# One fixed VectorE order behind attention, with weight conversion in portions, and a row of its own for token maxima

## The chip, the cores and the metric

The kernel runs on one core of one Trainium2 chip. The metric is the device time of one execution in microseconds (us), from three runs of the kernel before.

## The reference

Rotary attention over 4 batches, 8 heads, 576 positions and 64 dimensions gives 2304 tokens of 512 values; two feed-forward layers follow, here called expert 1 and expert 2 (512 to 2048 to 512). Cut to what matters:

```python
def _moe_ref(x, w_in, w_out, s, b):
    h = x @ w_in
    r = np.maximum(h, 0.0)
    g = s * (r * r) + b
    return (g @ w_out).astype(np.float32)

def _moe2_ref(x, w_in, w_out):
    h = x @ w_in
    g = h * (1.0 / (1.0 + np.exp(-1.702 * h)))
    return (g @ w_out).astype(np.float32)

def reference(**kwargs):
    attn_out = _attn_ref(**attn_kwargs)
    B, H, S, D = attn_out.shape
    x = np.ascontiguousarray(attn_out.transpose(0, 2, 1, 3)).reshape(B * S, H * D)
    x = _moe_ref(x=x, **moe_kwargs)
    return _moe2_ref(x=x, **moe2_kwargs)
```

The weights come as 64-bit floats and are turned into 32-bit ones on the chip.

## The kernel before, in words

**Stages.** Attention runs in 144 slots (to about 755 us); passes 0 to 7 of expert 1 are woven into it. `widen` (L1191) then frees attention's memory, and the rest, with which the change deals, follows: pass 8 of expert 1 (256 tokens, 755 to 805 us), pass 9 of expert 1 (512 tokens, 805 to 910 us, `LAST0` in the code), passes 10 to 13 of expert 2 (512 tokens each) and pass 14 (256 tokens, from 1295 us).

**Expert 1.** A pass has 16 blocks f of 128 hidden units. `first_layer` (L708) makes twelve matmuls into a bank `l`, then per 256 columns: ScalarE Relu from the bank (L723), VectorE times the bank again (L724: r*h, which is r*r), ScalarE scale and bias (L725), ScalarE copy to the high part (L726), VectorE subtraction for the low part (L727). `second_part` (L870) multiplies both parts into the `acc` banks two blocks later.

**Expert 2.** A pass has eight groups g of two blocks. `seven` (L816) computes both first-layer blocks with seven half-size products of half-precision pairs (a Strassen scheme): products 0, 3, 4, then 1, 2, 5, 6 with three or more `acc` matmuls in between (`between`, L1009). VectorE adds the products up (`add`, L836, tiles `u` and `c`; c1 is the half that is finished first), and product 6 is written into a bank that the sum after product 2 must have read. `gate` (L839) is ScalarE tanh (L842), VectorE multiply (L843), ScalarE copy (L844), VectorE subtraction (L845). The gate of the second half is put off into the next group (`then`, L1021).

**The next pass's tokens.** `sums_step` (L805), called once a group (in pass 9 once a block, f 5 to 12), prepares pass n+1: step 0 loads the tokens (`xr`), steps 1 and 2 take maxima on VectorE (L744, L752) and, in `share_top` (L556), store 128 maxima to memory (`tops`) and load them back as a row on all partitions (`top`), step 4 reduces that row and makes the scales (`scales`, L563 to L571, and L758) and lets GpSimd form differences, steps 5 to 7 split the result into half-precision pairs `xc` (L799 on ScalarE, L801 on VectorE). The row is a tile of the pair of buffers "r" that `seven` uses too, for `p` and `u`:

```python
row = moe.tile([128, TB], F32, tag="r", name=f"top{n}", bufs=2)
nc.sync.dma_start(row[:, 0:128], tops[n].partition_broadcast(128))
```

**Weight conversion of expert 2.** 32 raw tiles of 128x512 64-bit words (16 of each weight) go through three buffers "stage". `to_f32` (L480) costs one ScalarE operation (L483) and three VectorE operations (L484, L485, L488). `combine` (L590) takes two raw tiles to the seven weight matrices of a group: four GpSimd operations (L605), four ScalarE (L614), four VectorE (L615). `outer_pair` (L618) takes two raw tiles of the other weight: ScalarE copy (L630), GpSimd subtraction (L631) each. `refill` (L950) starts one whole such job after a block or group, in a fixed list of 16 jobs, when the buffer of expert 1's weights that it is to overwrite is free.

**What sets the order.** TensorE's order is written out (`pin`). VectorE, ScalarE, GpSimd and SP (the queue that issues all loads and stores, in order) get their order from the scheduler, which goes by priorities, readiness and free buffers; each engine then executes in that order and waits at the first instruction that is not ready. Through attention, 32 loads and maxima of expert 2's first weight (`top_load`, `top_max`, L544 to L554) are put into slots by the list `TOPS` (L1164).

## Time and profile before

| | us |
|---|---|
| three runs | 1346.38, 1350.62, 1354.55 |
| median | 1350.62 |
| the profiled execution, device time | 1356.49 |
| its span in the trace | 1354.7 |

The profiled execution is 5.9 us above the median and 1.8 us above its own span. The page gives each engine's busy time; the trace behind it lists instructions with start, length and what ended the idle time before. PE is TensorE, PEld its weight loads, DVE VectorE, ACT ScalarE, POOL GpSimd, SP the queue for transfers. A matmul of 512 columns is listed with its pipeline, so lengths of neighbours overlap.

### The profile page before, as it was taken

The numbers are of one execution on the slowest core, as the hardware profiler recorded it, in microseconds if no ns is written. First come the engines' busy times: TensorE is split into PE (matmuls) and PEld (weight loads), VectorE is DVE, ScalarE is ACT, GpSimd is POOL, SyncE is SP. The second block draws the span as 40 slices with busy tenths as digits, with TensorE's granted clock in tenths as the row PEclk, the third lists the DMA queues.
The fourth block names the chain that finished last, engine by engine and source line by source line (L and its number), as shares of the span: only waits on it lengthen the run. The fifth ranks groups of instructions, "written<-read, shape, count | busy, mean of one in ns | idle before, by whom it ended". The sixth has DMA issues, their size and how long they took to land.

```text
span 1354.7 us, 22515 instructions
## 1 busy us (share of the span) xinstructions
PE 1135.9 (84%) x8160; PEld 966.3 (71%) x8160; DVE 847.8 (63%) x1917; ACT 715.3 (53%) x1483; POOL 345.5 (26%) x363
## 2 busy tenths in 40 slices
PE   2665766898799799988999799786799797998998
PEld 1444555888798789988998797564576675776775
DVE  4978567785667665665664645889555464464554
ACT  1665665575666556665665555765333242342333
POOL 3547562153144144411111203335001001000000
PEclk9866888898899999999999899998899899999999
DMA  6687468697688766766652645544002002001010
GB/s 152 186 221 221 119 198 286 220 310 230 187 243 256 248 184 204 213 193 216 193 157 78 202 133 145 176 136 144 18 1 63 3 1 65 1 15 36 1 32 17
DMA packets 142879, 193.15 MB, mean 143 GB/s; under 512 B 32816, under 2 KB 105776, under 8 KB 142768
## 3 DMA queue, kind: packets, MB, share of 16 engines
q1 hardware_dynamic: 142768, 191.71, 47.3%
q8 instruction: 65, 1.06, 0.3%
q14 instruction: 46, 0.38, 0.1%
HBM read 146.05 MB, written 38.54 MB: 136 GB/s over the span
## 4 chain that ended last, share of the span: by engine, by line
PE 46%; DMA 19%; DVE 15%; ACT 4%; issue 4%; POOL 1%; SPq 1%; DVEq 0%; ACTq 0%; POOLq 0%
PE acc L99 20%; PE l L99 17%; DMA top<-in_moe_w_in_dram 5%; PE av L99 3%; DMA raw<-in_moe_w_in_dram 3%; PE s L99 3%; PE t L99 3%; DMA tops<-xm 2%; DVE P L394 2%; DMA stages<-in_moe_w_in_dram 1%; DMA top<-tops 1%; DVE pt L437 1%; DMA vm<-in_v_dram 1%; DVE wc L615 1%; DVE g L727 1%
## 5 line engine op out<-in xcount | busy, mean ns | idle before, releaser
L99 PE MATMUL acc<-wo,g 128*128 128x512 f32 x864 | 255.8, 422 | 5.7 <-DVE g L845 3.9
L99 PE MATMUL l<-xc,wc 128*128 128x256 f16 (+1 forms) x1680 | 203.4, 266 | 40.5 <-DVE c L836 25.7
L414 POOL TENSOR_SCALAR P<-P,st 128x576 f32<-128x576 f32 x144 | 120.4, 837 | 382.1 <-DVE st L413 251.0
L99 PEld LDWEIGHTS <-wc 128*128 128x128 f16 x1680 | 139.3, 99 | 107.7 <-issue 94.6
L99 PEld LDWEIGHTS acc<-wo,g 128*128 128x128 f32 x864 | 152.8, 195 | 34.6 <-DVE g L845 7.0
L99 PE MATMUL acc<-g,w 128*128 128x256 f32 (+1 forms) x1056 | 164.6, 306 | 5.3 <-DVE g L727 3.5
L99 PEld LDWEIGHTS acc<-g,w 128*128 128x128 f32 x1056 | 145.6, 197 | 13.0 <-DVE g L727 5.0
L403 ACT ACTIVATE P<-P,st 128x576 f32<-128x576 f32 x144 | 111.8, 776 | 78.2 <-DVE P L394 77.9
L99 PE MATMUL t<-ident,P 128*128 128x128 f32 x720 | 113.6, 293 | 44.1 <-POOL P L414 17.6
L394 DVE TENSOR_SCALAR_CACHE_REDUCE P<-s 128x576 f32<-128x576 f32 x144 | 108.3, 752 | 65.5 <-PE s L99 61.1
L99 PE MATMUL l<-xh,w 128*128 128x256 f32 x616 | 128.9, 292 | 13.5 <-DVE r L724 11.2
L842 ACT ACTIVATE r<-c 128x512 f32<-128x512 f32 (+1 forms) x80 | 47.0, 588 | 153.9 <-DVE c L836 125.7
L99 PEld LDWEIGHTS t<-ident,P 128*128 128x128 f32 x720 | 87.7, 151 | 54.9 <-POOL P L414 26.8
L99 PEld LDWEIGHTS l<-xh,w 128*128 128x128 f32 x616 | 103.6, 195 | 15.9 <-DVE r L724 14.8
L437 DVE TENSOR_TENSOR pt<-t,pt 128x640 f16<-128x640 f32 x120 | 98.4, 820 | 23.8 <-ACT pt L435 23.2
L435 ACT CAST pt<-t 128x640 f16<-128x640 f32 x144 | 98.8, 686 | 23.1 <-PE t L99 22.6
L725 ACT ACTIVATE r<-r,sb 128x256 f32<-128x256 f32 x144 | 86.6, 602 | 46.0 <-DVE r L724 45.7
L99 PE MATMUL s<-k,qb 128*128 128x320 f32 x480 | 89.2, 313 | 9.8 <-DVE P L394 8.5
L99 PE MATMUL l<-xl,w 128*128 128x256 f32 x308 | 88.4, 287 | 0.0
L727 DVE TENSOR_TENSOR g<-r,g 128x256 fp32r<-128x256 f32 x144 | 69.5, 482 | 28.6 <-ACT g L726 25.9
L99 PEld LDWEIGHTS s<-k,qb 128*128 128x128 f32 x480 | 73.9, 196 | 17.9 <-DVE P L394 10.6
L843 DVE SCALAR_TENSOR_TENSOR r<-r,c 128x512 f32<-128x512 f32 (+1 forms) x80 | 52.2, 653 | 44.6 <-ACT r L842 44.6
(145 smaller groups left out, 2025.6 us busy)
## 6 DMA issues: line engine op xcount, KB each, us to landing
ws<-wd SPq DMA_DIRECT2D x80, 512.0 KB, 4.6
k<-ksp SPq DMA_DIRECT2D x24, 576.0 KB, 6.0
top<-in_moe_w_in_dram SPq DMA_DIRECT2D x32, 256.0 KB, 3.8
raw<-in_moe_w_in_dram SPq DMA_DIRECT2D x16, 512.0 KB, 5.1
rawo<-in_moe_w_out_dram SPq DMA_DIRECT2D x16, 512.0 KB, 3.3
wd<-w SPq DMA_DIRECT2D x10, 512.0 KB, 5.0
nat<-in_k_dram SPq DMA_DIRECT2D x16, 288.0 KB, 4.5
nat<-in_q_dram SPq DMA_DIRECT2D x16, 288.0 KB, 4.7
```

The costliest lines, as they stand in the source:

```text
L99: pin(nc.tensor.matmul(*args, **kw))
L394: nc.vector.tensor_scalar(pr, ps[:, 192 : 192 + S], -Q_SCALE, None, op0=ALU.mult, op1=ALU.min, accum_out=st[:, 0:1],)
L403: nc.scalar.activation(pr, pr, AF.Exp, bias=st[:, 0:1], scale=-1.0, accum_out=st[:, 1:2])
L414: nc.gpsimd.tensor_scalar(pr, pr, st[:, 2:3], 1.0, op0=ALU.mult, op1=ALU.mult)
L435: nc.scalar.copy(hi, pc)
L437: nc.vector.tensor_tensor(lo, pc, hi, op=ALU.subtract)
L615: nc.vector.scalar_tensor_tensor(lo, src, col, hi, op0=ALU.mult, op1=ALU.subtract)
L725: nc.scalar.activation(r, r, AF.Identity, bias=sb[:, 1:2], scale=sb[:, 0:1])
L727: nc.vector.tensor_tensor(gl[:, cols], r, f32(gh[:, cols]), op=ALU.subtract)
L842: nc.scalar.activation(r, c, AF.Tanh, scale=0.851)
L843: nc.vector.scalar_tensor_tensor(r, r, 1.0, c, op0=ALU.add, op1=ALU.mult)
```

## The change

- **VectorE's order.** From `widen` on, every VectorE instruction is chained in the order in which the code is written (`dv`), with no semaphore. ScalarE's part of a conversion is kept behind the last chained one (`pace`).
- **Conversion in portions.** `combine` and `outer_pair` become generators that hand out a cost after each VectorE operation; `convert(budget)` takes portions: 1.8 per block of pass 8, 3.5 per block of pass 9, and 2.5, 0.8 and 1.5 at three places of each group. Raw tiles are loaded ahead, up to three alive (`fill`); an outer pair's job starts only when its buffer is free.
- **Token maxima.** The row is now 256 half-precision columns at the end of the tile `xc`, allocated at step 0; `sums_step` moves into the group, behind the sum after product 4.
- **Gates.** The second gate is no longer put off; it multiplies in place (c, not r).
- **Square.** In passes 8 and 9 the product L724 becomes a ScalarE Square.
- **Attention.** The 32 maxima loads go to every third slot from 40 to 133; the row of the weights' maximum moves from the buffers "r" to "V".

```diff
+    def dv(ins):
+        if late:
+            pin(ins, "dve")
+        return ins
...
-        nc.scalar.activation(f32(high), f32(high), AF.Copy, scale=2.0**-112)
-        nc.vector.tensor_scalar(low, low, 29, None, op0=ALU.logical_shift_right)
+        pace(nc.scalar.activation(f32(high), f32(high), AF.Copy, scale=2.0**-112))
+        dv(nc.vector.tensor_scalar(low, low, 29, None, op0=ALU.logical_shift_right))
+        yield 0.55
...
-    def share_top(n, col):
+    def share_top(n, col, row):
         nc.sync.dma_start(tops[n], col)
-        row = moe.tile([128, TB], F32, tag="r", name=f"top{n}", bufs=2)
-        nc.sync.dma_start(row[:, 0:128], tops[n].partition_broadcast(128))
-        return row
+        nc.sync.dma_start(row, tops[n].partition_broadcast(128))
...
+    def fill():
+        for job in [r for r in raws if "t" not in r]:
+            if live[0] == 3:
+                return
+            g, i, m = job["at"]
+            job["t"] = late["m2"].tile([128, 512], U64, tag="stage", name=f"raw{m}{g}{i}", bufs=3)
+            stage_load(job["t"], w_in2, w_out2, 2 * g + i, m)
+            live[0] += 1
...
-            nc.vector.tensor_tensor(r, r, ps[:, cols], op=ALU.mult)
+            if late:
+                nc.scalar.activation(r, r, AF.Square)
+            else:
+                nc.vector.tensor_tensor(r, r, ps[:, cols], op=ALU.mult)
...
+        xc = late["m2"].tile([128, 14 * T + 256], F16, tag="xc", name=f"xc{n}", bufs=2)
+        x["xc"] = xc[:, 0 : 14 * T].rearrange("p (j z t) -> p j z t", j=7, z=2)
+        x["row"] = xc[:, 14 * T : 14 * T + 256].bitcast(F32)
...
         add(cb[:, half:T], b1, u2)
-        then()
+        side(0)
         between()
...
         add(cb[:, half:T], a1, cb[:, half:T])
+        side(1)
         between()
         product(5, b1, False, True)
         add(cb[:, 0:half], b1, u2)
-        ready_b(*gate(cb, 1))
+        gb = gate(cb, 1)
         between()
         product(6, a1, False, True)
         add(ca[:, half:T], a1, u2)
-        return lambda: gate(ca, 0)
+        low(gb, cb)
+        ga = gate(ca, 0)
+        low(ga, ca)
+        side(2)
+        return ga, gb
...
+            if late:
+                convert(3.5 if T == 512 else 1.8)
...
+                def side(i):
+                    if i == 0 and n + 1 < len(PASSES):
+                        sums_step(ahead.setdefault(n + 1, {}), n + 1, g)
+                    convert((2.5, 0.8, 1.5)[i])
...
-    TOPS = [*range(58, 68), *range(94, 104), *range(122, 134)]
-    for i, x in enumerate(TOPS):
-        at(x, top_load, i)
-        at(x + 2, top_max, i)
+    for i in range(32):
+        at(40 + 3 * i, top_load, i)
+        at(42 + 3 * i, top_max, i)
```

**Where instructions move.** Names carry pass and group: u11_4 belongs to pass 11, group 4; the last digit of c11_41 is 1 for the half that is finished first.

VectorE, pass 11, before: the reduction of the row (L564) stands in group 2, in front of the sum after product 2 (c11_21 from l12).

```order
L752 TENSOR_REDUCE xm12_11423<-xm12_11423 128x1
L836 SCALAR_TENSOR_TENSOR u11_2_11524<-l10_8998,xm11_10634,p11_2_11523 128x256
L843 SCALAR_TENSOR_TENSOR r11_10_11546<-r11_10_11546,c11_10_11426 128x512
L836 SCALAR_TENSOR_TENSOR c11_21_11522<-l11_8999,xm11_10634,u11_2_11524 128x256
L845 TENSOR_TENSOR g11_10_11547<-r11_10_11546,g11_10_11547 128x512
L564 TENSOR_REDUCE xm12_11423<-top2_11614 128x1
L565 TENSOR_SCALAR xm12_11423<-xm12_11423 128x1
L566 TENSOR_SCALAR xm12_11423<-xm12_11423 128x1
L836 SCALAR_TENSOR_TENSOR c11_21_11522<-l12_9000,xm11_10634,c11_21_11522 128x256
```

VectorE, pass 11, after the change:

```order
L904 TENSOR_TENSOR g11_30_11692<-c11_30_11620,g11_30_11692 128x512
L893 SCALAR_TENSOR_TENSOR u11_4_11712<-l10_8998,xm11_10459,p11_4_11711 128x256
L893 SCALAR_TENSOR_TENSOR c11_41_11710<-l11_8999,xm11_10459,u11_4_11712 128x256
L592 TENSOR_REDUCE xm12_11349<-xc12_11350 128x1
L593 TENSOR_SCALAR xm12_11349<-xm12_11349 128x1
L595 TENSOR_SCALAR xm12_11349<-xm12_11349 128x1
L599 RECIPROCAL xm12_11349<-xm12_11349 128x1
L600 TENSOR_SCALAR xm12_11349<-xm12_11349 128x1
L601 TENSOR_SCALAR xm12_11349<-xm12_11349 128x1
L832 TENSOR_SCALAR xm12_11349<-xm12_11349,wscale_109 128x1
L893 SCALAR_TENSOR_TENSOR c11_41_11710<-l12_9000,xm11_10459,c11_41_11710 128x256
```

The reduction (now L592, from the tail of xc) has moved from group 2 to group 4, behind the sum after product 4; the maxima (L826) are still taken in group 2.

VectorE, pass 10, group 2, before (rawo70 and raw70 are raw tiles under conversion):

```order
L836 SCALAR_TENSOR_TENSOR u10_2_10753<-l10_8998,xm10_9935,p10_2_10752 128x256
L485 SCALAR_TENSOR_TENSOR rawo70_10731<-rawo70_10731 128x512
L836 SCALAR_TENSOR_TENSOR c10_21_10751<-l11_8999,xm10_9935,u10_2_10753 128x256
L845 TENSOR_TENSOR g10_11_10703<-r10_11_10702,g10_11_10703 128x512
L488 SCALAR_TENSOR_TENSOR rawo70_10731<-rawo70_10731 128x512
L615 SCALAR_TENSOR_TENSOR wc7_10607<-raw70_10608,wscale_109,wc7_10607 128x2x256
L615 SCALAR_TENSOR_TENSOR wc7_10607<-raw71_10614,wscale_109,wc7_10607 128x2x256
L564 TENSOR_REDUCE xm11_10634<-top1_10843 128x1
L843 SCALAR_TENSOR_TENSOR r10_10_10775<-r10_10_10775,c10_10_10637 128x512
```

and after the change (rawTrue is the second weight, rawFalse the first):

```order
L893 SCALAR_TENSOR_TENSOR u10_2_10672<-l10_8998,xm10_9896,p10_2_10671 128x256
L893 SCALAR_TENSOR_TENSOR c10_21_10670<-l11_8999,xm10_9896,u10_2_10672 128x256
L817 TENSOR_REDUCE xm11_10459<-xr11_1_10458 128x1 x2
L826 TENSOR_REDUCE xm11_10459<-xm11_10459 128x1
L500 TENSOR_SCALAR rawTrue51_10647<-rawTrue51_10647 128x512
L503 SCALAR_TENSOR_TENSOR rawTrue51_10647<-rawTrue51_10647 128x512
L509 SCALAR_TENSOR_TENSOR rawTrue51_10647<-rawTrue51_10647 128x512
L500 TENSOR_SCALAR rawFalse60_10665<-rawFalse60_10665 128x512
L893 SCALAR_TENSOR_TENSOR c10_21_10670<-l12_9000,xm10_9896,c10_21_10670 128x256
L503 SCALAR_TENSOR_TENSOR rawFalse60_10665<-rawFalse60_10665 128x512
L893 SCALAR_TENSOR_TENSOR c10_21_10670<-l11_8999,xm10_9896,u10_2_10672 128x256
L899 SCALAR_TENSOR_TENSOR c10_21_10670<-r10_21_10741,c10_21_10670 128x512
```

A raw tile of group 5 is now converted in one piece between the sums of group 2, where before the conversion of group 7's tiles stood; the whole list of jobs lies later.

ScalarE, pass 9, block 6, before:

```order
L723 ACTIVATE r9_60_9955<-l10_8998 128x256
L614 ACTIVATE wc3_9908<-raw30_9909,wscale_109 128x2x256
L483 ACTIVATE raw31_9915<-raw31_9915 128x512
L725 ACTIVATE r9_60_9955<-r9_60_9955,sb_86 128x256
L723 ACTIVATE r9_61_9961<-l10_8998 128x256
L726 CAST g9_6_9954<-r9_60_9955 128x256
L725 ACTIVATE r9_61_9961<-r9_61_9961,sb_86 128x256
L483 ACTIVATE rawo20_9980<-rawo20_9980 128x512
L614 ACTIVATE wc3_9908<-raw31_9915,wscale_109 128x256
L726 CAST g9_6_9954<-r9_61_9961 128x256
```

and after the change:

```order
L789 ACTIVATE r9_60_9929<-l10_8998 128x256
L789 ACTIVATE r9_61_9935<-l10_8998 128x256
L791 ACTIVATE r9_60_9929<-r9_60_9929 128x256
L791 ACTIVATE r9_61_9935<-r9_61_9935 128x256
L794 ACTIVATE r9_60_9929<-r9_60_9929,sb_86 128x256
L794 ACTIVATE r9_61_9935<-r9_61_9935,sb_86 128x256
L795 CAST g9_6_9928<-r9_60_9929 128x256
L795 CAST g9_6_9928<-r9_61_9935 128x256
L499 ACTIVATE rawTrue11_9906<-rawTrue11_9906 128x512
```

The two Squares (L791) are new between Relu and scale; no instruction of VectorE stands in this chain any more up to the copy.

## Rows read from the trace of the kernel before

**Rows 1.** Page, part 1: busy time, share of the span, instructions.

```profile
PE 1135.9 (84%) x8160; PEld 966.3 (71%) x8160; DVE 847.8 (63%) x1917; ACT 715.3 (53%) x1483; POOL 345.5 (26%) x363
```

**Rows 2.** Stretches: length, PE, PEld, DVE, ACT, POOL busy (instructions), PE clock, DMA, GB/s.

```profile
755.00:805.00 50.00, 44.52 (x353) 43.66 (x352) 30.58 (x56) 29.32 (x61) 7.90 (x8) 0.97 0.51 162
805.00:910.40 105.40, 91.48 (x388) 71.85 (x387) 78.79 (x142) 67.09 (x141) 35.24 (x31) 0.97 0.47 144
910.40:1019.40 109.00, 87.84 (x529) 66.07 (x528) 72.54 (x130) 48.58 (x87) 20.76 (x17) 0.92 0.18 60
1019.40:1295.40 276.00, 252.27 (x1585) 192.14 (x1584) 140.94 (x274) 96.00 (x178) 14.69 (x12) 0.96 0.09 23
```

**Rows 3.** The same view, one undisturbed group of pass 11.

```profile
1062.56:1072.80 10.24, 10.24 (x68) 7.85 (x67) 4.22 (x8) 3.31 (x6) 0.00 (x0) 1.00 0.01 2
```

**Rows 4.** PE in order of time, two blocks of pass 9: start, length, what.

```profile
888.62 2.88 PE L99 MATMUL l<-x,w 128*128 128x512 f32 x12
894.06 2.88 PE L99 MATMUL l<-x,w 128*128 128x512 f32 x12
```

**Rows 5.** DVE in order of time, pass 11, group 2; last the wait before.

```profile
1055.64 0.29 DVE L564 TENSOR_REDUCE xm<-top 128x1 f32<-128x128 f32 x1 [8.56 <-DMA top<-tops]
1056.22 0.48 DVE L836 SCALAR_TENSOR_TENSOR c<-l,xm,c 128x256 f32<-128x256 f32 x1
```

**Rows 6.** SP's issues, same stretch.

```profile
1044.11 0.33 SPq L558 DMA_DIRECT2D tops<-xm  x1
1051.19 0.33 SPq L560 DMA_DIRECT2D top<-tops  x1
```

**Rows 7.** PE, same stretch.

```profile
1056.75 1.44 PE L99 MATMUL l<-xc,wc 128*128 128x256 f16 x6 [7.83 <-DVE c L836]
1057.84 4.88 PE L99 MATMUL acc<-wo,g 128*128 128x512 f32 x12
```

**Rows 8.** PE's waits, 1019.4 to 1295.4: total, times, longest.

```profile
PE l L99 <- DVE c L836: 20.8, 3, 8.0
```

**Rows 9.** PE's waits, 910.4 to 1019.4.

```profile
PE l L99 <- DVE xm L566: 7.1, 1, 7.1
```

**Rows 10.** DVE groups by line, 910.4 to 1019.4: busy, mean ns, idle before.

```profile
L615 DVE SCALAR_TENSOR_TENSOR wc<-raw,wscale,wc 128x512 f16<-128x512 f32 x6 | 5.1, 860 | 0.0
L485 DVE SCALAR_TENSOR_TENSOR rawo<-rawo 128x512 uint32<-128x512 uint32 x5 | 3.5, 694 | 0.3 <-ACT rawo L483 0.3
L488 DVE SCALAR_TENSOR_TENSOR rawo<-rawo 128x512 uint32<-128x512 uint32 x5 | 3.5, 691 | 0.0
L484 DVE TENSOR_SCALAR rawo<-rawo 128x512 uint32<-128x512 uint32 x5 | 3.2, 635 | 1.4 <-DMA rawo<-in_moe_w_out_dram 1.4
```

**Rows 11.** DVE in order of time, one group of pass 10 without conversion.

```profile
986.02 0.69 DVE L843 SCALAR_TENSOR_TENSOR r<-r,c 128x512 f32<-128x512 f32 x1 [0.76 <-ACT r L842]
988.79 0.69 DVE L843 SCALAR_TENSOR_TENSOR r<-r,c 128x512 f32<-128x512 f32 x1 [0.70 <-ACT r L842]
```

**Rows 12.** Tile raw: how long its loads take.

```profile
DMA to landing us min/median/max: 3.8/5.1/10.1
```

**Rows 13.** POOL groups by line, 910.4 to 1019.4.

```profile
L631 POOL TENSOR_TENSOR wo<-rawo,wo 128x512 fp32r<-128x512 f32 x5 | 6.9, 1388 | 35.6 <-ACT wo L630 35.6
```

**Rows 14.** ACT groups by line, 805 to 910.

```profile
L630 ACT CAST wo<-rawo 128x512 fp32r<-128x512 f32 x11 | 7.2, 661 | 4.7 <-DVE rawo L488 4.6
```

**Rows 15.** PE's waits, 805 to 910.4.

```profile
PE l L99 <- DVE r L724: 6.5, 4, 2.5
```

**Rows 16.** ACT groups by line, from 1295.4 on.

```profile
L842 ACT ACTIVATE r<-c 128x256 f32<-128x256 f32 x16 | 6.7, 417 | 21.3 <-DVE c L836 17.9 <-DVE g L845 3.4
```

**Rows 17.** DVE groups by line, 805 to 910.

```profile
L724 DVE TENSOR_TENSOR r<-r,l 128x256 f32<-128x256 f32 x30 | 12.4, 413 | 7.5 <-ACT r L723 7.5
```

**Rows 18.** PE's waits, 755 to 805.

```profile
PE l L99 <- DVE r L724: 5.5, 4, 2.1
```

**Rows 19.** Waits of all engines, 200 to 760.

```profile
DVE wmax L553 <- DMA top<-in_moe_w_in_dram: 24.8, 21, 2.5
```

More of the change, by code (lines that the diff above doesn't have):

```diff
@@ L478, with pace @@
     stages = []
+    def dv(ins):
+        if late:
+            pin(ins, "dve")
+        return ins
+    def pace(ins):
+        if "dve" in chains:
+            tc.add_manual_dep(
+                ins.ins,
+                chains["dve"],
+                mybir.DependencyInfo(
+                    mybir.DependencyClass.NoSync, mybir.DependencyReason.SCHED_ONLY
+                ),
+                reason="pace",
+            )
     def to_f32(raw):
@@ L579, in top_send @@
         )
-        wtop["row"] = share_top(7, col)
+        wtop["row"] = att.tile([128, 128], F32, tag="V", name="wrow", bufs=2)
+        share_top(7, col, wtop["row"])
     def top_scale():
@@ L588, with take, done_with, flush @@
     outer = {}
+    raws = []
+    live = [0]
+    after = []
+    def fill():
[6 more added lines that the diff above has]
+            live[0] += 1
+    def take():
+        fill()
+        return raws.pop(0)["t"]
+    def done_with(n):
+        live[0] -= n
+        fill()
+    def flush():
+        while after:
+            try:
+                cost = next(after[0])
+            except StopIteration:
+                after.pop(0)
+                continue
+            yield cost
+    def halves(wc, parts):
+        for cs, src, col in parts:
+            hi, lo = wc[:, cs, 0], wc[:, cs, 1]
+            pace(nc.scalar.activation(hi, src, AF.Copy, scale=col))
+            dv(nc.vector.scalar_tensor_tensor(lo, src, col, hi, op0=ALU.mult, op1=ALU.subtract))
+            yield 0.7
     def combine(g, tag):
@@ L594, in combine @@
         for i in range(2):
-            raw = late["m2"].tile([128, 512], U64, tag="stage", name=f"raw{g}{i}", bufs=3)
-            stage_load(raw, w_in2, w_out2, 2 * g + i, 0)
-            two.append([z.rearrange("p (k f) -> p k f", k=2) for z in to_f32(raw)])
+            got = yield from to_f32(take())
+            two.append([z.rearrange("p (k f) -> p k f", k=2) for z in got])
+            if i == 0:
+                yield from flush()
         (aa, s12), (ab, s34) = two
@@ L626, in outer_pair @@
                 o = t[:, 2 * i : 2 * i + 2]
-            raw = late["m2"].tile([128, 512], U64, tag="stage", name=f"rawo{g}{i}", bufs=3)
-            stage_load(raw, w_in2, w_out2, 2 * g + i, 1)
-            low, high = to_f32(raw)
-            nc.scalar.copy(o[:, 0], low)
+            low, high = yield from to_f32(take())
+            pace(nc.scalar.copy(o[:, 0], low))
             nc.gpsimd.tensor_tensor(o[:, 1], low, f32(o[:, 0]), op=ALU.subtract)
-            outer[g].append(o)
+            outer.setdefault(g, []).append(o)
+            done_with(1)
+            yield from flush()
     def split3(o, prods, first, last):
@@ L814, in sums_step, with seven @@
             sums_split(x, 3 if i == 5 else 2)
-    def seven(n, g, x, between, then, ready_b):
+    def seven(n, g, x, between, side):
         T = PASSES[n][2]
@@ L997, in experts @@
                 yield
-            refill()
             if n == LAST0:
@@ L1016, in experts @@
             for g in range(NG):
-                while jobs and (jobs[0][1] <= g or jobs[0][0] is outer_pair and jobs[0][1] <= g):
-                    refill()
-                late_b = []
-                def then():
-                    if behind:
-                        m, f, fn = behind.pop()
-                        queue.extend(parts_of(m, f, outer[f // 2][f % 2], *fn()))
-                def ready_b(gh, gl):
-                    late_b.extend(parts_of(n, 2 * g + 1, outer[g][1], gh, gl))
-                behind.append((n, 2 * g, seven(n, g, x, between, then, ready_b)))
+                need(g, combos)
+                if after:
+                    for cost in flush():
+                        pass
+                if g:
+                    need(g - 1, outer)
+                def side(i):
+                    if i == 0 and n + 1 < len(PASSES):
+                        sums_step(ahead.setdefault(n + 1, {}), n + 1, g)
+                    convert((2.5, 0.8, 1.5)[i])
+                ga, gb = seven(n, g, x, between, side)
                 yield
@@ L1032, in experts @@
                     between()
[L1033 removed]
+                need(g, outer)
+                for i, g2 in ((1, gb), (0, ga)):
+                    queue += parts_of(n, 2 * g + i, outer[g][i], g2[:, 0], g2[:, 1])
                 yield
[L1035 to L1039 removed]
         while queue:
```

164 lines of the change are left out of this document (85 added, 79 removed).

## The prediction

> **What bounds the kernel now.** I read the page first: TensorE is busy for 84% of the span and no other engine above 63% [rows 1]. Then the trace cut into stretches, since the change acts mainly behind attention, from 755 us on [rows 2]. The reader should compare each stretch with what TensorE needs when nothing holds it. In passes 11 to 13 an undisturbed group takes 10.24 us, all of it TensorE at full clock, with VectorE busy for 4.22 and ScalarE for 3.31 [rows 3]. 24 such groups are 245.8 us, but the stretch lasts 276.0 [rows 2]: 30.2 us are lost. In pass 9 two starts of the same matmul batch lie 5.44 us apart [rows 4], so 16 blocks need 87.0; the stretch lasts 105.4. Pass 10 needs 8 groups, 81.9 us, and lasts 109.0. So some 76 us in three stretches are waits, or matmuls at the lower clock behind waits.
>
> Next, what the waits are. In passes 11 to 13 TensorE waits 20.8 us in three waits for a sum of VectorE [rows 8]. One of them, seen from VectorE: it sits idle for 8.56 us at the reduction L564 for the row `top`, and only behind that comes the sum for which TensorE waits [rows 5]. SP shows why the row is late: the store of the maxima was issued at 1044.11, the load of the row only at 1051.19, and VectorE started at 1055.64 [rows 6, 5]: 11.5 us for the round trip. The reduction stands so early because the row lies in a pair of buffers that group 3 needs again. TensorE then waits for 7.83 us, and its next twelve `acc` matmuls are listed with 4.88 us [rows 7] against 2.88 [rows 4]: it came back at the lower of its two levels of clock (1.2 and 2.4 GHz). Pass 10 has the same wait, 7.1 us [rows 9].
>
> **The change, part by part.**
>
> *The row of its own.* It removes the reason for the early reduction. By the orders shown, the maxima are still taken in group 2 and the reduction now stands in group 4, two groups or 20.5 us later, against a round trip of 11.5. What remains in passes 11 to 13 is 10.24 us per group. VectorE's own work there is unchanged and covered (4.22 of 10.24). The gain is between 20.8 (the idle time alone) and 30.2 (with what the clock costs behind it); I take 30, since groups that nothing disturbs run without any gap. That each token load is now issued ahead of the previous pass's output stores on SP costs nothing: those stores have a whole pass to land.
>
> *Pass 10.* VectorE is busy here for 72.5 us. The new order leaves 12 raw tiles and the last step of a thirteenth where 9 were converted before, and 12 multiplications for `wc` where there were 8. That adds 3 x 0.64 + 3 x 0.69 + 4 x 0.69 + 4 x 0.86 = 10.2 us [rows 10], in all 82.7. The last group has no conversion, so (82.7 - 4.2) / 7 = 11.2 us per group in the other seven: above TensorE's 10.24, so VectorE becomes the bound here. In a fixed order it also sits through ScalarE's part of each gate, 0.76 + 0.70 us per group [rows 11], which the scheduler's order could fill with conversion: 12.7 per group, 88.7 for seven, 98.9 with the last. The pair's second raw tile is another hold: its buffer comes free when the ScalarE copy (0.66) [rows 14] and the GpSimd subtraction (1.39) [rows 13] of the first are done, and its load takes 5.1 [rows 12], together 7.15 us, while only two `wc` multiplications, two sums and two maxima stand between. This comes three times in pass 10. Ends: 88.7 without any hold (7 x 11.2 + 10.24), 120.4 with all three loads late by 7.15. I take 101, nearer to the first end because several microseconds of work and of waiting for products do stand in between: 109 - 101 = 8 us gained, of which 7.1 are the row's wait.
>
> *Square in passes 8 and 9.* VectorE loses 32 instructions of 0.413 us in pass 9 [rows 17], and bank `l` is now free after Relu. TensorE's waits for the old product, 6.5 us in pass 9 [rows 15] and 5.5 in pass 8 [rows 18], lose their cause. ScalarE gains 32 x 0.417 = 13.3 us (0.417 is the price of a tanh on the same shape) [rows 16], on 67.1: 80.4 of the 87.0 that TensorE needs. VectorE goes from 78.8 to 65.6 with the conversion of 16 raw tiles as before. So TensorE would again set the pace, with little room on ScalarE. Pass 9 cannot gain more than 18.4 (105.4 - 87.0) and may gain nothing; TensorE's busy time there is 91.5, 4.5 above its need, which is the clock. I take 6.5 and half of 4.5: 9 us. In pass 8 I take 4 of 5.5, since a conversion now stands, by the fixed order, in front of a subtraction that attention's last block needs; ends 5.5 gained and 5.1 lost (one load) [rows 12].
>
> The Trainium skill ("ScalarE: Activation LUTs", section on rules for kernel authors) says the opposite of this part: multiplication belongs on VectorE, not on ScalarE. By that rule the Square would bring nothing in passes 8 and 9 and the sum below would be 13 us higher; the rows bear out neither side yet, since VectorE and ScalarE are within 12 us of each other there [rows 2]. The same page prices an activation with fixed scale at 186 ns plus 0.833 ns per element, an estimate of 0.40 us here, beside the row's 0.417.
>
> *Gates no longer put off, pass 14.* VectorE's work is the same. The second gate now ends before the next group's first sum; its result is needed a group later. I cost it at nothing; if the cover is gone, 8 groups x 0.417 [rows 16] = 3.3 us lost.
>
> *Attention.* Loads of 32 tiles move from three bursts to every third slot. VectorE waits 24.8 us for them [rows 19], but TensorE mostly waits for others. They now share two buffers with the value loads. I take 0, with 8 us (a third of 24.8) either way. The last row in "V" frees a buffer of first-layer results for a moment: nothing.
>
> **The sum.** 30 + 8 + 9 + 4 = 51 us less than the profiled execution's 1356.5, thus 1305.5; that execution lies 5.9 above the median of the runs, so a median of about 1300 us is forecast. All best ends together give 82 us less, all worst ends 7 more.
>
> **The rivals.**
> - *Late raw loads.* All three second tiles of pass 10 come late by 7.15 (120.4 instead of 101) and pass 9 gains nothing, because sums and subtractions stand behind a conversion whose load has not landed. For: three buffers, as before. Against: loads are asked for earlier. -30 + 11 + 0 - 4 = -23, or 1328 us.
> - *ScalarE becomes the bound in passes 8 and 9.* Its conversions fall into 13 of the 16 blocks, so 80.4 of 87.0 may be over the limit there. Then both gains vanish: -38, or 1313 us. This is what the skill's rule would make of it.
> - *Slower: SP holds the loads.* SP waits 7.1 us between the store of the maxima and the load of the row [rows 6], with raw loads behind it; before, VectorE could do something else meanwhile. If all 12 tiles of pass 10 come late by 7.15, it takes 98.9 + 86 = 185, and the result is 1300 + 84 = 1384 us. It decides for slower from eight late tiles on (51 / 7.15 = 7.1). Against: one store per pass.
> - *The row is late all the same.* If SP's stores hold the row by over 9 us (20.5 - 11.5), the waits of passes 11 to 13 return: 1330 us.
>
> **How the numbers follow.** The forecast has 0.60, late loads 0.18, ScalarE 0.14, the late row 0.04, SP's hold 0.04. The likeliest is 1300 us. The range is 1278 to 1330: down by 22 us, some 0.7 of the 31 that the best ends leave beyond the forecast (82 - 51), since not all of them come together; up to the late-load and late-row cases. A measurement here tells changes of about 0.5% (6.8 us) from none. All cases but SP's hold lie well below 1344: faster 0.93, the same 0.03, slower 0.04.
>
> **What would show it.** Right: no idle time of VectorE at the row's reduction in passes 11 to 13, groups of 10.24 us there, about 246 us for 24 of them; pass 10 near 101 with VectorE its busiest engine; no TensorE wait on a product in passes 8 and 9, ScalarE near 80 us in pass 9. Wrong: VectorE idle before L500 for a raw load, several times 5 us or more, with TensorE waiting for sums behind it; or Relu starting late in pass 9 behind conversions; or attention ending later than 755 us.

## The result, and the profile after

| | us |
|---|---|
| kernel before, median of 4 runs here | 1350.20 |
| changed kernel, median of 4 runs (1312.59 to 1318.78) | 1313.52 |
| ratio, 95% interval | 0.9735 (0.9696 to 0.9775) |

The change makes the kernel faster by 36.7 us (2.7%): inside the range of 1278 to 1330, with the sign forecast, but 13.5 us short of 1300. The profiled execution of the changed kernel took 1312.85 us. Part 1 of its page answers to [rows 1]:

```profile
PE 1129.1 (86%) x8160; PEld 968.0 (74%) x8160; DVE 837.3 (64%) x1868; ACT 729.7 (56%) x1532; POOL 344.2 (26%) x363
```

The stretches, cut at the same matmuls as in [rows 2] (the first one behind attention, the first of pass 9, of pass 10, of pass 11, of pass 14); columns as there:

```profile
759.50:811.75 52.25, 49.82 (x409) 49.21 (x410) 22.93 (x38) 38.22 (x84) 7.00 (x8) 1.00 0.60 205
811.75:899.98 88.23, 86.43 (x387) 71.34 (x385) 65.30 (x106) 69.91 (x167) 28.21 (x25) 0.98 0.46 156
899.98:1006.50 106.52, 88.84 (x528) 67.60 (x528) 83.25 (x145) 54.40 (x99) 28.07 (x24) 0.94 0.25 85
1006.50:1252.30 245.80, 245.80 (x1587) 188.20 (x1585) 143.03 (x274) 96.80 (x177) 13.97 (x12) 1.00 0.09 21
1252.30:1311.10 58.80, 52.31 (x457) 37.69 (x456) 26.26 (x73) 21.26 (x55) 0.00 (x0) 0.99 0.12 28
```

Attention is not in that view. Its last transposed matmul batch, in TensorE's order of time, in the kernel before and in the changed one (start, length, what, wait before it):

```profile
739.86 1.93 PE L99 MATMUL av<-pt,vf 128*64 128x320 f16 x25 [0.40 <-DVE pt L437]
```

```profile
757.01 1.93 PE L99 MATMUL av<-pt,vf 128*64 128x320 f16 x25 [0.40 <-DVE pt L437]
```

From one profiled execution to the other the stretches moved by these amounts (pass 8 from the first block behind attention, 742.4 and 759.5, to the first batch of pass 9, 805.1 and 811.8):

| stretch | before | after | moved | forecast |
|---|---|---|---|---|
| attention and the passes woven in | 742.4 | 759.5 | +17.1 | 0, at most 8 either way |
| pass 8 | 62.7 | 52.2 | -10.5 | -4 |
| pass 9 | 105.3 | 88.2 | -17.1 | -9 |
| pass 10 | 109.0 | 106.5 | -2.5 | -8 |
| passes 11 to 13 | 276.0 | 245.8 | -30.2 | -30 |
| pass 14 | 59.3 | 58.8 | -0.5 | 0 |

The sum is -43.7, from an execution of before that lay some 6 us above its median, to one of the changed kernel that lay at its median; the medians differ by 36.7.

Passes 11 to 13 are as forecast: 245.8 us, TensorE busy for all of it, clock 1.00. VectorE's order of time in pass 11 shows why. The last maximum ends at 1031.6, the reduction stands 19 us later and has no wait in front of it (compare [rows 5]):

```profile
1031.41 0.16 DVE L826 TENSOR_REDUCE xm<-xm 128x1 f32<-128x4 f32 x1
...
1050.22 0.27 DVE L592 TENSOR_REDUCE xm<-xc 128x1 f32<-128x128 f32 x1
```

SP's issues there. The round trip itself is what it was, 7.2 us from store to load [rows 6]; in passes 11 to 13 nobody waits for it any more:

```profile
1031.60 0.34 SPq L588 DMA_DIRECT2D tops<-xm  x1
1038.75 0.33 SPq L589 DMA_DIRECT2D xc<-tops  x1
```

All of TensorE's waits, in pass 9 and in passes 11 to 14 (us in total, times, longest):

```profile
PE acc L99 <- DVE g L796: 1.8, 1, 1.8
```

```profile
PE acc L99 <- ACT g L900: 0.7, 1, 0.7
```

Before, the waits of passes 11 to 14 were 24.5 us, of which 20.8 are [rows 8]. Those of pass 9 were 13.9 us: 6.5 for the product [rows 15] and these:

```profile
PE acc L99 <- DVE g L727: 4.1, 3, 2.1
PE acc L99 <- ACT g L726: 1.9, 2, 1.7
PE acc L99 <- DVE xm L566: 1.4, 1, 1.4
```

**Attention is where the rest went.** VectorE's order of time near its end, in the changed kernel:

```profile
646.43 0.08 DVE L394 DVE_READ_ACCUMULATOR P<-s 128x1 f32 x1
656.70 0.29 DVE L592 TENSOR_REDUCE wscale<-wrow 128x1 f32<-128x128 f32 x1 [10.19 <-DMA wrow<-tops]
...
657.49 0.14 DVE L410 TENSOR_SCALAR st<-st 128x1 f32<-128x1 f32 x1
```

and SP's issues:

```profile
644.46 0.32 SPq L588 DMA_DIRECT2D tops<-wscale  x1
651.97 0.32 SPq L589 DMA_DIRECT2D wrow<-tops  x1
```

This is the wait of [rows 5] over again, at another place. The row here is that of the weights' maximum, which the change moved from the buffers "r" to "V". VectorE reaches its reduction (L592, the same function) at 646.5 and stands there for 10.19 us, because SP issued the load of the row 7.5 us behind the store and the load takes 4.7. Behind it stands L410, the work of a softmax. In the kernel before, the store was issued at 646.08 and the load only at 699.78, when the buffer of "r" came free (SP's waits there, first row), and the reduction stood further back in VectorE's order, where it met a row that had landed (second row, VectorE in order of time, no wait in front of it):

```profile
SPq L560 <- DVE g L727: 5.9, 1, 5.9
```

```profile
702.61 0.28 DVE L564 TENSOR_REDUCE wscale<-top 128x1 f32<-128x128 f32 x1
```

**Pass 10.** VectorE is busy for 83.3 us, as forecast (82.7). TensorE is listed with more, 88.8 us at a mean clock of 0.94, but it waits for VectorE's sums:

```profile
PE l L99 <- DVE c L893: 15.5, 8, 3.4
```

VectorE's longest waits there, and that for raw tiles:

```profile
DVE g L904 <- ACT g L900: 8.1, 15, 1.2
DVE c L899 <- ACT r L898: 6.1, 9, 0.8
...
DVE rawTrue L500 <- DMA rawTrue<-in_moe_w_out_dram: 1.3, 2, 0.8
```

It waits 14.2 us for ScalarE's part of the gates and 1.3 us for loads.

### The profile page after: what moved, and what is told of

Read it like the earlier page. It is cut to its first block, busy times and chain, and to the rows that moved or that the text cites. A ratio compares the mean times of both kernels' runs of the same rounds, so it can differ in the third digit from the quotient of the medians.

```text
span 1311.1 us, 22610 instructions
## 1 busy us (share of the span) xinstructions
PE 1129.1 (86%) x8160; PEld 968.0 (74%) x8160; DVE 837.3 (64%) x1868; ACT 729.7 (56%) x1532; POOL 344.2 (26%) x363
## 4 chain that ended last, share of the span: by engine, by line
PE 53%; DVE 13%; DMA 11%; ACT 6%; issue 3%; POOL 1%; SPq 0%; DVEq 0%; ACTq 0%; POOLq 0%
PE acc L99 23%; PE l L99 20%; DMA top<-in_moe_w_in_dram 4%; PE av L99 4%; PE s L99 3%; PE t L99 3%; DMA stages<-in_moe_w_in_dram 2%; DVE P L394 2%; DVE pt L437 1%; DVE g L796 1%; ACT r L794 1%; ACT P L403 1%; DMA stage<-in_moe_w_in_dram 1%; DMA x<-part 1%; ACT pt L435 1%
## 5 line engine op out<-in xcount | busy, mean ns | idle before, releaser
L414 POOL TENSOR_SCALAR P<-P,st 128x576 f32<-128x576 f32 x144 | 123.1, 856 | 396.3 <-DVE st L413 255.9
L99 PE MATMUL l<-xc,wc 128*128 128x256 f16 (+1 forms) x1680 | 200.0, 264 | 17.7 <-DVE c L893 15.5
L437 DVE TENSOR_TENSOR pt<-t,pt 128x640 f16<-128x640 f32 x120 | 98.3, 819 | 21.4 <-ACT pt L435 20.9
L796 DVE TENSOR_TENSOR g<-r,g 128x256 fp32r<-128x256 f32 x144 | 73.5, 520 | 47.4 <-ACT g L795 45.1
L789 ACT ACTIVATE r<-l 128x256 f32<-128x256 f32 x144 | 52.7, 375 | 55.6 <-PE l L99 48.8
```

The costliest lines, as they stand in the source:

```text
L99: pin(nc.tensor.matmul(*args, **kw))
L414: nc.gpsimd.tensor_scalar(pr, pr, st[:, 2:3], 1.0, op0=ALU.mult, op1=ALU.mult)
L437: nc.vector.tensor_tensor(lo, pc, hi, op=ALU.subtract)
L789: nc.scalar.activation(r, ps[:, cols], AF.Relu)
L796: dv(nc.vector.tensor_tensor(gl[:, cols], r, f32(gh[:, cols]), op=ALU.subtract))
```

## The experiments

Eleven kernels in three sets (e1 to e4, e5 to e8, e9 to e11), each timed beside the kernel before on the same chip, which took 1348.8, 1349.7 and 1349.9 us in them; each kernel has four runs, e1 ten. Stage lengths of each profiled execution, in us; pass 10 here ends with the first sum of pass 11, which is 1.6 to 1.9 us later than the stretch above.

| run | time, median | ratio to before (95%) | attention | pass 8 | pass 9 | pass 10 | 11 to 13 |
|---|---|---|---|---|---|---|---|
| before | 1350.2 | 1 | 742.4 | 62.7 | 105.3 | 110.7 | 275.5 |
| changed | 1313.5 | 0.974 (0.970 to 0.978) | 759.5 | 52.2 | 88.2 | 108.4 | 245.3 |
| e1 | 1345.9 | 0.999 (0.996 to 1.001) | 736.4 | 62.4 | 100.9 | 107.9 | 278.1 |
| e2 | 1312.1 | 0.973 (0.970 to 0.975) | 737.5 | 61.7 | 101.3 | 104.0 | 247.2 |
| e3 | 1303.4 | 0.966 (0.963 to 0.969) | 746.7 | 54.9 | 86.4 | 109.2 | 245.3 |
| e4 | 1295.3 | 0.960 (0.956 to 0.964) | 739.0 | 51.7 | 89.8 | 112.2 | 245.3 |
| e5 | 1329.3 | 0.983 (0.979 to 0.987) | 732.1 | 62.1 | 111.3 | 115.1 | 245.3 |
| e6 | 1303.9 | 0.965 (0.961 to 0.969) | 737.1 | 59.7 | 101.1 | 98.0 | 247.9 |
| e7 | 1291.6 | 0.954 (0.948 to 0.959) | 739.6 | 54.8 | 89.9 | 103.4 | 245.3 |
| e8 | 1313.4 | 0.972 (0.968 to 0.975) | 738.2 | 52.3 | 101.5 | 116.3 | 245.2 |
| e9 | 1308.3 | 0.966 (0.961 to 0.971) | 740.8 | 56.1 | 99.4 | 109.9 | 245.3 |
| e10 | 1285.6 | 0.952 (0.947 to 0.956) | 736.3 | 51.7 | 89.1 | 101.9 | 245.3 |
| e11 | 1295.3 | 0.958 (0.952 to 0.964) | 738.9 | 56.0 | 92.0 | 104.8 | 245.2 |

All but "changed" and e3 have VectorE's order of before in attention. Their attention stretches still lie between 732.1 and 742.4: they differ by up to 10 us there with nothing changed in that order.

### e1 and e2: the buffer or the place in the order

Both start from the kernel before. e1 gives the row its place in xc and changes nothing else; e2 adds one ordering edge.

```diff
+        xc = late["m2"].tile([128, 14 * T + 256], F16, tag="xc", name=f"xc{n}", bufs=2)
+        x["xc"] = xc[:, 0 : 14 * T].rearrange("p (j z t) -> p j z t", j=7, z=2)
+        x["tail"] = xc[:, 14 * T : 14 * T + 256].bitcast(F32)
...
-            x["row"] = share_top(x["n"] - LAST0 - 1, m[:, 4:5])
+            x["row"] = share_top(x["n"] - LAST0 - 1, m[:, 4:5], x["tail"])
```

```diff
-        nc.vector.tensor_reduce(down, row[:, 0:128], axis=AX.X, op=ALU.max)
+        ins = nc.vector.tensor_reduce(down, row[:, 0:128], axis=AX.X, op=ALU.max)
+        if late:
+            behind_sum(ins)
```

> The kernel before with one part of the change alone: the row of the maxima lies at the end of xc instead of in the pair of buffers r. VectorE's order is still the scheduler's, and it still puts the reduction of the row into group 2, right behind the maxima. Theory A (it is the place of the reduction in VectorE's order that costs, the buffer is only one reason for that place): nothing gained in passes 11 to 13, 276 us again, three waits of TensorE of 7 to 8 us or less, total 1345 to 1355. Theory B (the shared buffers themselves hold the row, by a late load): the waits go, passes 11 to 13 take 246 us, total about 1313 to 1318.

> The kernel before with the row in xc and one ordering edge more: in passes 10 to 14 the reduction of the row stands behind the last sum of group 4. Nothing else of the change. Theory A: passes 11 to 13 take 246 us as in the change, pass 10 loses its wait of 7.1 us, total 1350 - 30 - 7 = 1313 to 1318, that is the whole of what the change gives; then portions, Square and the fixed order together are worth nothing net, because what they gain in passes 8 and 9 (27 us) is lost in attention (17 us) and pass 10. Rival: the fixed order of all of VectorE's instructions is what removes the waits, and one edge leaves others: passes 11 to 13 above 255 us.

e1 gained nothing (1345.9 us, same). VectorE's waits of e1 from 1000 to 1300 us, and TensorE's:

```profile
DVE xm L565 <- DMA xc<-tops: 27.8, 3, 10.0
```

```profile
PE l L99 <- DVE c L838: 23.6, 3, 8.4
```

The row has a place of its own, and VectorE still stands before its reduction three times, 27.8 us in all, because the scheduler puts it into group 2. e2, with the edge, took 1312.1 us, the time of the whole change. The same view of TensorE in e2, and the reduction of pass 11 (start, length, no wait before it):

```profile
PE acc L99 <- DVE g L849: 1.4, 2, 0.9
```

```profile
1053.23 0.28 DVE L565 TENSOR_REDUCE xm<-xc 128x1 f32<-128x128 f32 x1
```

What costs is the place of the reduction in VectorE's order; the row's own buffer only allows a later place. The fixed order of all other instructions isn't needed for this: with the one edge passes 11 to 13 are 28.3 us shorter, with the whole change 30.2.

The edge works from pass 10 on, where the sums begin; in pass 9 the reduction of e1 and e2 has no such edge. VectorE stands 10.8 us before it there in both. In the kernel before it did not wait at all: the shared buffer kept the load back (store at 819.72, load at 861.88), and the reduction at 869.83 met a row that had landed. So a buffer of its own moves the reduction forward in pass 9, and costs a wait there.

### e3 and e4: what attention lost

Both start from the changed kernel. e3 puts the weights' row back into "r"; e4 also puts the 32 loads back into three bursts.

```diff
-        wtop["row"] = att.tile([128, 128], F32, tag="V", name="wrow", bufs=2)
+        wtop["row"] = moe.tile([128, TB], F32, tag="r", name="wrow", bufs=2)[:, 0:128]
```

```diff
-    for i in range(32):
-        at(40 + 3 * i, top_load, i)
-        at(42 + 3 * i, top_max, i)
+    TOPS = [*range(58, 68), *range(94, 104), *range(122, 134)]
+    for i, x in enumerate(TOPS):
+        at(x, top_load, i)
+        at(x + 2, top_max, i)
```

> The changed kernel with the row of the weights' maximum back in the buffers r, as before, so that its reduction goes back behind some 88 more VectorE instructions. Theory A: the wait of 10.2 us at that reduction goes, and attention ends 6 to 8 us earlier than in the change (last matmul av at 749 to 751 instead of 757), total 1305 to 1308. Rival: other work of attention fills in nothing and the late loads of the 32 tiles hold it all the same: attention ends within 2 us of 757, total 1312 to 1315.

> The changed kernel with attention as before in both points: the row of the weights' maximum in the buffers r, and the 32 loads in their three bursts. Theory A (the 17 us that attention lost come from these two edits): the last matmul av at 740 to 742 as before, total 1296 to 1299, and the difference to the run with the row alone, some 9 us, is what the spreading of the loads costs. Rival (attention's time moves by several us with any change of the scheduler's order, whichever edit): the last av at 747 or later, total above 1303.

The last matmul batch of attention in e3, and in e4:

```profile
744.20 1.93 PE L99 MATMUL av<-pt,vf 128*64 128x320 f16 x25 [0.40 <-DVE pt L437]
```

```profile
736.43 1.93 PE L99 MATMUL av<-pt,vf 128*64 128x320 f16 x25 [0.40 <-DVE pt L437]
```

Against 757.01 in the changed kernel, e3 gains 12.8 us there and e4 another 7.8. In e3 the row's load is again issued late (704.12, its store at 641.59), and the reduction stands where it hardly waits:

```profile
707.30 0.29 DVE L592 TENSOR_REDUCE wscale<-wrow 128x1 f32<-128x128 f32 x1 [0.27 <-DMA wrow<-tops]
```

The medians fall by 10.1 and 8.2 (1313.5, 1303.4, 1295.3): together 18 us are the price of the two edits, some 10 of the row's early reduction and some 8 of the spread loads. Executions differ by up to 10 us in attention, as said above, so the medians are the better measure; the intervals of e3 and e4 just overlap, so the second price is the less sure. Both runs came out faster than expected, by 1.6 and 0.8 us beyond the ranges. Which waits make up the 8 us is not shown; VectorE's own waits for the maxima loads (200 to 760 us, as in [rows 19]) are 33.8 us in e3 and 21.4 in e4.

### e5 and e6: Square, portions, and the fixed order

e5 is e4 with the product back on VectorE, in its fixed order. e6 is e2 with Square as the one other part.

```diff
-            if late:
-                nc.scalar.activation(r, r, AF.Square)
-            else:
-                nc.vector.tensor_tensor(r, r, ps[:, cols], op=ALU.mult)
+            dv(nc.vector.tensor_tensor(r, r, ps[:, cols], op=ALU.mult))
```

> The kernel with attention as before (the run before this, 1295.25 us), and in passes 8 and 9 the product r*r back on VectorE, in its fixed order, instead of Square on ScalarE. Theory A (the Square is what took TensorE's waits in passes 8 and 9 away): the waits on the product are back, pass 9 takes 96 to 105 us instead of 89.8, the stretch from attention's last av to pass 9 58 us or more instead of 54.3, total 1305 to 1318. Theory B (the fixed order with small portions does it, whoever multiplies; VectorE would be busy for 65.3 + 13 = 78 of 87 us): pass 9 within 3 us of 89.8, total 1293 to 1300.

> The kernel before with the row behind the sum of group 4 (run e2, 1312 us), and Square on ScalarE in passes 8 and 9 as the one other part; the scheduler still sets the order and whole tiles are converted at a time. Theory A (Square alone is enough): pass 9 falls from 101.3 to 88 to 93 us, total 1298 to 1304. Theory B (portions are needed too): pass 9 stays at 97 or more, total 1307 to 1313. The skill's rule (multiplication on VectorE) would have it at 1313 or above.

e5 lost 34 us against e4, in its profiled execution 21.5 in pass 9 and 10.4 in pass 8: more than theory A. It is slower in pass 9 than the kernel before was (111.3 against 105.3). Waits of TensorE and VectorE in e5, 795 to 912 us:

```profile
PE l L99 <- DVE r L790: 17.8, 10, 4.5
```

```profile
DVE g L793 <- ACT g L792: 38.3, 32, 2.0
```

In a fixed order VectorE stands before each of the 32 subtractions until ScalarE has scaled and copied (38.3 us in all). With the product on VectorE, the next product, for which TensorE's bank waits, is queued behind that. With Square the bank depends on ScalarE alone.

e6 gained 8.3 us against e2, but none of it in pass 9 (101.1 against 101.3). TensorE's waits of e6, 796.75 to 897.87 us, are now for other results:

```profile
PE acc L99 <- DVE g L733: 6.0, 5, 2.7
PE acc L99 <- ACT g L732: 5.5, 1, 5.5
```

So neither theory was right as a whole. e5 shows that the fixed order with portions does not give pass 9 its 88 to 90 us without Square. What e6 lacks is less clear, for it differs from e4 in more than the portions. It has no fixed order, its loads are not asked for ahead, and in its pass 9 VectorE stands at the row's reduction as in e1 and e2. ScalarE waits for the scale behind that, and TensorE's wait of 5.5 us for ScalarE follows:

```profile
823.68 0.29 DVE L565 TENSOR_REDUCE xm<-xc 128x1 f32<-128x128 f32 x1 [8.61 <-DMA xc<-tops]
```

Which of these holds e6 at 101.1 us isn't shown. What e6 gained lies in pass 10 (98.0 against 104.0) and pass 8.

### e7: portions inside the gates

e4 with two places more for portions.

```diff
             nc.scalar.activation(r, c, AF.Tanh, scale=0.851)
+            if z:
+                side(3)
...
-        low(ga, ca)
         side(2)
+        low(ga, ca)
...
-                    convert((2.5, 0.8, 1.5)[i])
+                    convert((1.8, 0.8, 1.5, 0.7)[i])
```

> The kernel with attention as before (1295.25 us), and conversion portions placed into the two places of each group where VectorE waits for ScalarE's part of the gate: one before the first multiplication by 1 + tanh, and the last portion before the last subtraction. The budgets are 1.8, 0.8, 0.7 and 1.5 instead of 2.5, 0.8 and 1.5, the same sum within 0.0. In the change VectorE waits 14.2 us for ScalarE's gate in pass 10. Theory A (VectorE is the bound of pass 10, and these waits are part of it): pass 10 shorter by 6 to 9 us, total 1286 to 1290. Theory B (TensorE's waits come from the portions that stand ahead of the sums, and VectorE's idle time only moves): less than 2 us, total 1293 to 1297.

VectorE's waits for ScalarE's gate in pass 10 of e4, and of e7:

```profile
DVE g L904 <- ACT g L900: 12.0, 15, 3.5
DVE c L899 <- ACT r L898: 6.1, 9, 0.8
```

```profile
DVE g L906 <- ACT g L902: 5.0, 10, 1.7
...
DVE c L901 <- ACT r L898: 2.4, 5, 0.9
```

They fell by 10.7 us (in the changed kernel they were 14.2), and pass 10 from 112.2 to 103.4: theory A for the stretch. Of the total only 3.6 us are seen (1291.6, just above the range of theory A), and the intervals of e4 and e7 overlap, so a gain in the total isn't shown; pass 8 of the profiled execution was 3.0 longer.

### e8, e9, e10, e11: more conversion in pass 9, and SP's hold

e8 is e4 with 4.3 instead of 3.5 per block of pass 9. e9 is e8 with the row's load one step behind its store, e10 is e7 with that, and e11 is e10 with 3.9.

```diff
-                convert(3.5 if T == 512 else 1.8)
+                convert(4.3 if T == 512 else 1.8)
```

```diff
-            share_top(x["n"] - LAST0 - 1, m[:, 4:5], x["row"])
+            nc.sync.dma_start(tops[x["n"] - LAST0 - 1], m[:, 4:5])
...
+        elif i == 3:
+            pace(nc.sync.dma_start(x["row"], tops[n - LAST0 - 1].partition_broadcast(128)))
```

> The kernel with attention as before (1295.25 us), and a budget of 4.3 instead of 3.5 per block of pass 9, so that 9 raw tiles instead of 12 and a third are left for pass 10. Theory A (pass 10 is bound by VectorE's work, pass 9 by TensorE): some 9 us of VectorE's work leave pass 10, it is shorter by 7 to 9 us, pass 9 stays within 2 us of 89.8, total 1286 to 1290. Theory B (pass 9 has no room left, VectorE and ScalarE wait for each other there): pass 9 longer by as much as pass 10 gains, total 1293 to 1298.

> Run e8 (budget 4.3 in pass 9, 1313.4 us) with one difference: the load of the row of maxima is issued one step later than the store, so that raw loads may stand between the two on SP. In e8 SP waited 6.9 us between store and row load with three raw loads behind it, VectorE waited 8.4 us for the first of them, and TensorE 5.7 us behind that. Theory A (SP's hold is what made e8 slow): that wait goes, pass 9 falls from 101.5 to 90 to 96 us, total 1299 to 1307. Theory B (three buffers for raw tiles are too few for 4.3 per block, the hold only showed it): the wait goes to another raw tile, pass 9 stays above 98, total 1310 or more.

> Run e7 (portions within the gates, budget 3.5 in pass 9, 1291.6 us) with the load of the row one step later. In e7 no raw load of pass 9 was late, VectorE waited 1.7 us for raw tiles in pass 10. So by theory A of e9 little is to be had here: 1288 to 1293 us; by theory B nothing, the same range; above 1295 would say that the later row load costs something of its own at the reduction.

> Run e10 with a budget of 3.9 per block in pass 9 instead of 3.5, half way to 4.3. Theory A (loads were the only thing against more conversion in pass 9): some 4 us of VectorE's work leave pass 10, total 1284 to 1290. Theory B (raw tiles come late as soon as pass 9 converts faster): 1294 or more.

e8 lost 18 us. SP's issues, VectorE and TensorE in order of time, in pass 9 of e8:

```profile
842.24 0.32 SPq L588 DMA_DIRECT2D tops<-xm  x1
849.51 0.32 SPq L589 DMA_DIRECT2D xc<-tops  x1
849.94 2.23 SPq L530 DMA_DIRECT2D rawTrue<-in_moe_w_out_dram  x3
```

```profile
856.64 0.43 DVE L500 TENSOR_SCALAR rawTrue<-rawTrue 128x512 uint32<-128x512 uint32 x1 [8.44 <-DMA rawTrue<-in_moe_w_out_dram]
```

```profile
859.46 4.54 PE L99 MATMUL acc<-g,w 128*128 128x512 f32 x12 [5.68 <-ACT g L795]
```

ScalarE stands at the same tile (its waits, 790 to 905 us):

```profile
ACT rawTrue L499 <- DMA rawTrue<-in_moe_w_out_dram: 9.2, 4, 7.3
```

The row's load waits for the store, three raw loads stand behind it, VectorE sits 8.44 us and ScalarE 7.3 at the first step of a tile, and TensorE waits 5.68 for a result of ScalarE queued behind that, and comes back with twelve matmuls in 4.54 us instead of 2.88 [rows 4], at a mean granted clock of 0.64, so mostly at the lower level. But SP's hold is only about half of the 8.44 us. A raw load also needs one of the three buffers. In e9 the same load goes out at 852.06, when VectorE's last multiplication for `wc` but one has ended (851.25 + 0.74). In e8 that one ends at 845.57:

```profile
844.82 0.75 DVE L654 SCALAR_TENSOR_TENSOR wc<-rawFalse,wscale,wc 128x512 f16<-128x512 f32 x1
```

So the hold kept the first raw load back by 4.4 us, to 849.94. The other half is the load itself, 6.6 us long and asked for when VectorE had little work left. And 5.7 of TensorE's 11.7 us of waits in this pass lie behind that tile; the other 6.0 are five waits for VectorE's subtraction. In the changed kernel, at 3.5 per block, VectorE did not wait for a raw tile in pass 9.

e9 was 5 us faster than e8, of the 18. The waits of VectorE and TensorE that answer to these two, and SP's at the row's load, 790 to 905 us:

```profile
DVE rawTrue L500 <- DMA rawTrue<-in_moe_w_out_dram: 6.6, 3, 5.6
```

```profile
PE acc L99 <- ACT g L795: 3.9, 1, 3.9
```

```profile
SPq L868 <- DMA tops<-xm: 4.2, 1, 4.2
```

The longest wait for a raw tile fell by 2.8 us and is still 5.6, though its load now goes out as soon as its buffer is free; pass 9 is still 99.4. SP issues one raw load ahead of the row's load and two behind it, so the hold is not quite gone. The intervals of e8 and e9 overlap, so e9 settles little: theory A holds for a part at most, theory B for the stretch.

e10 came out at 1285.6, below the range expected. In its pass 9 SP still waits 7.3 us at the row's load, with no raw load in between, and the first one behind it goes out at 842.31, when VectorE's multiplication has freed its buffer: the hold cost nothing there, and the step changed nothing about it. e11 was slower than e10 by the medians, by 2.9 us in pass 9 and 2.9 in pass 10. Its total is in theory B's range, but not by theory B's mechanism: VectorE waited only 0.9 us for raw tiles in its pass 9. The intervals of e10 and e11 overlap. What holds pass 9 above 3.5 per block stays open.

**e10 beats both kernels**: 1285.6 us, ratio 0.952, 28 us less than the changed kernel. It is the changed kernel with attention as before, portions within the gates, and the row's load one step later. That this last step gains by itself isn't shown (e7 and e10 overlap).

## Why the prediction was right, and where its terms were off

1. *The row of its own: right in size, half right in reason.* 30 us were forecast for passes 11 to 13 and 30.2 came, with groups of 10.24 us and no wait at the reduction. The prediction said that the reduction stands early "because the row lies in a pair of buffers that group 3 needs again", and that the row of its own "removes the reason". e1 shows that this alone removes nothing: the scheduler has it early without that reason too. The gain came from the place in the fixed order, which the prediction read from the orders shown, and e2 has 28.3 of it with one edge.
2. *Attention: the step that failed.* "They now share two buffers with the value loads. I take 0" and "The last row in "V" frees a buffer of first-layer results for a moment: nothing". The stretch lost 17.1 us, over twice the 8 allowed either way, and one of the prediction's own signs of being wrong came: attention ended later than 755 us. The row cost some 10 us (e3) and the loads some 8 (e4). The second sentence looked at the buffer given free, and not at what the buffer had held back: in "r" the row's load came late, and so its reduction came late in VectorE's order. In "V" the scheduler put it right behind the store, and VectorE paid the same round trip as in passes 11 to 13. The mechanism was the prediction's own, found in one place and not looked for in the second, though the new order would have shown it.
3. *Pass 9: too small.* 9 us were taken between 0 and 18.4, and 17.1 came, almost the upper end. The term was mis-sized because it counted only the waits for the product, 6.5 us, and half of the clock's 4.5. All of TensorE's waits fell, from 13.9 us to 1.8, and its busy time by 5.1. How much of the other waits went with Square, and how much with the order, the portions and the earlier loads, isn't shown: VectorE waited 14.0 us for raw loads in pass 9 before, and not at all in the changed kernel. ScalarE was not near its limit: 69.9 us busy in 88.2, not 80.4 of 87.0. 4.3 us of that is conversion, whose four groups there sum to 24.3 us, and to 28.6 in the kernel before. More than half of the rest is how the price was used: Square is listed with 0.414 us, as forecast, but the listed lengths of neighbours overlap. Two Squares at 840.31 are followed by the next instruction at 840.93, 0.31 us each. The rival of ScalarE as the bound falls with that. e5 adds what the prediction didn't see: the order and the portions do not give this without Square.
4. *Pass 8: too small.* 4 us were taken and 10.5 came. From the first block behind attention on, TensorE waited 10.6 us before and 3.0 after; the forecast knew 5.5 of this, since its cut at 755 us put a wait of 4.5 for the product into attention. The other 2.9 are TensorE's busy time, at a granted clock of 0.95 before and 1.00 after.
5. *Pass 10: too large.* 8 us were taken and 2.5 came, though VectorE's work was sized well (82.7, measured 83.3). The term that failed is its idle time: 101 - 82.7 = 18.3 us were taken, 23.3 came. I took some 2 us of late raw loads; VectorE waited 1.3 us for them. I took 0.76 + 0.70 us for ScalarE's part of the gates in seven groups, 10.2; it was 14.2 in the stretch, and e7 shows that this was to be had: with 10.7 us less of it than in e4 the stretch was 8.8 shorter. "VectorE its busiest engine" did not come, by listed time: TensorE has 88.8 us, 83.3 are VectorE's.
6. *The rivals.* Late raw loads and SP's hold did not decide here. At 4.3 per block raw loads did come late (e8), and the hold was a part of that, 4.4 us before a wait of 8.44. The late row fell. The rival of ScalarE had 1313 us, the time that came, but by chance: it has both gains in passes 8 and 9 vanish, and they were 27.6 us.

The sum was right to 14 us by luck: passes 8 and 9 gained 15 us more than forecast, attention lost 17 and pass 10 fell short by 5.5. That leaves the sum 7 us short; the other 6 are that the forecast took off what the profiled execution of before lay above its median, while that of the changed kernel lay at its own.

The Trainium skill ("ScalarE: Activation LUTs", section on rules for kernel authors) has multiplication on VectorE, for a price per element that it gives for 16-bit operands with one source. Here, with 32-bit operands and two sources, it was the other way: the two prices are alike (0.413 on VectorE [rows 17], 0.414 on ScalarE), and with the product in VectorE's fixed order the kernel was 34 us slower (e5); in the scheduler's order it was 8 us slower (e2 against e6). What decided was not the price but which engine's queue the product stood in.

## What to carry to other kernels

When a transfer's result is late, look first at where its consumer stands in the engine's order: moving the buffer alone may change nothing (e1), while one ordering edge may give it all (e2). A buffer that is shared can also hold something back usefully, as in attention and in pass 9 of e1 and e2; whoever gives it away should look in the new order at what moves forward with it. An in-order queue that waits between a store and its load holds every load behind it. What that costs is counted from the moment when such a load could have gone out, not from the whole wait that follows: 4.4 us of 8.44 in e8.

## What the runs showed of the hardware

VectorE's conversion instructions can take two to four times as long while GpSimd works. VectorE and GpSimd in pass 10 of the changed kernel, in order of time, and the same two VectorE instructions where no GpSimd instruction was under way when they began (the next is listed from 964.19 on):

```profile
915.44 1.51 DVE L500 TENSOR_SCALAR rawFalse<-rawFalse 128x512 uint32<-128x512 uint32 x1
917.06 1.59 DVE L503 SCALAR_TENSOR_TENSOR rawFalse<-rawFalse 128x512 uint32<-128x512 uint32 x1
```

```profile
915.28 1.39 POOL L847 TENSOR_TENSOR xt<-xr 128x512 f32<-128x512 f32 x1 [6.32 <-DMA x<-y]
916.75 1.35 POOL L847 TENSOR_TENSOR xt<-xr,xt 128x512 f32<-128x512 f32 x1
```

```profile
963.49 0.42 DVE L500 TENSOR_SCALAR rawFalse<-rawFalse 128x512 uint32<-128x512 uint32 x1
964.01 0.69 DVE L503 SCALAR_TENSOR_TENSOR rawFalse<-rawFalse 128x512 uint32<-128x512 uint32 x1
```

L500 takes 1.51 instead of 0.42 us, L503 1.59 instead of 0.69, ending 0.3 and 0.5 us behind a GpSimd instruction. The Trainium skill ("SBUF — State Buffer", section "SBUF: two separate sides") has the two engines share a pair of ports, which VectorE needs in its modes with two ports or for two operands from this memory; whichever starts first holds it for a whole instruction, while the other blocks. The trace agrees. The means that the prediction used for the conversion (0.64 for the first step) already held such cases.

A load that needs a store of 128 single values holds SP for long: in the changed kernel SP issues the row's load 7.2 to 7.9 us behind the store, in all of passes 9 to 13; before, it was 7.1 in pass 11 [rows 6].
